# Two of the first loads issued by ScalarE, and one warm-up matmul fewer

## The chip, the cores and the metric

The kernel runs on one core of a Trainium2 chip. The metric is the device time of one execution in microseconds (us), smaller is better. A difference is told in per cent of the time before.

## What is computed

`x` is 2048 x 512. The output mixes two branches of `x`, row by row, with a gate. All of it is float32.

```
g = sigmoid((x * gate_w).sum(-1))
# branch A: real part of a DFT along the hidden and the sequence dimension
a = x @ dft_hid_re.T;  b = x @ dft_hid_im.T
A = dft_seq_re @ a - dft_seq_im @ b
# branch B: a gated MLP with ReLU, 512 -> 1792 -> 512
B = (relu(x @ W_gate) * (x @ W_up)) @ W_down
out = g * A + (1 - g) * B
```

## The kernel before

Every float32 operand is split in a high and a low part, and a product is made of three matmuls (high by low, low by high, high by high), each 128 x 128 by 128 x 512. Most products go through a scheme of seven half-size products per 2 x 2 block product. Only the first block of the MLP is multiplied directly (class `Direct`), so that its matmuls need little preparation. In the trace these matmuls write `c` from `xb11h`, `xb11l`, `xb21h` and so on (parts of `x`) and from `wf0h`, `wf0l`, `wf1h`, `wf1l` (parts of the first weight tile; 0 and 1 are the two values of `d`).

The program is recorded first. Each step gets a key, which is its due place in the row of matmuls. A planner then decides in which order each engine runs its steps, and which of 51 SBUF units each buffer gets. TensorE (PE) runs its matmuls in the order written. VectorE (DVE) and ScalarE (ACT) may take steps out of turn by due time, and so may the queue of SyncE (SP), which issues the loads. The planner reckons with a queue for each engine that issues DMAs.

The head of the program is what the change touches. PE runs `WARM` matmuls on a memset tile (`warm`, which has no other use) while the first data are loaded. SP issues `x` "11" (two pieces, `k` 0 and 1, 256 KB each) and the first weight tile `wf` with `d` 0 (two pairs of 128 KB for each `k`), in the order x, wf, wf, x, wf, wf, and then the pieces for `d` 1. VectorE casts each piece of x "11" to `xb11h` and subtracts to get `xb11l`. ScalarE casts each pair of `wf` to `wf0h`, and VectorE subtracts to get `wf0l`. The first real matmul needs `xb11h` and the first pair of `wf0h`, both for `k` 0. The third and fourth need the second pair, and the next four need `xb11l`.

Of the kernel before, what the change touches and what calls it, by code (L numbers as in the profile page):

```python
# [344 lines left out]
def kernel(ctx: ExitStack, tc, xP, xG, wf, wgu, wd, cr, ci, wri, gw, out):  # L345
# [27 lines left out]
    plan = Plan()  # L373
# [20 lines left out]
    def buf(name, shape=(2, N), dtype=F32):  # L394
        return Buf(plan, name, list(shape), dtype)
# [22 lines left out]
    def mm(ps, w, x, start=False, stop=False):  # L418
        plan.tensor.matmul(ps, w, x, start=start, stop=stop, skip_group_check=True)
# [7 lines left out]
    def load(o, i):  # L427
        plan.sync.dma_start(o, i)
# [187 lines left out]
    class Direct:  # L616
# [32 lines left out]
                   start=first, stop=d == k == 1 and n == 2)  # L649

        def w_load(self, d, k, s=slice(0, 4)):
            load(self.raw[d][:, k, s], wf[d, :, k, s])

        def w_hi(self, d, k, s=slice(0, 4)):
            E().scalar.copy(self.w[d][0][:, k, s], self.raw[d][:, k, s])
# [624 lines left out]

    WARM = 8
    warm, wp = buf("warm", [P], F32R), Pair("warm")

    def warm_up():
        E().vector.memset(f32(warm.all), 1.0)
        wp.new()
        for n in range(WARM):
            mm(wp[0], warm.all, warm.all.unsqueeze(1).to_broadcast([P, N // P, P]), start=n == 0, stop=n == WARM - 1)  # L1290

# [180 lines left out]
```

## Time and profile before

| | |
|---|---|
| time, median of 3 runs | 783.7 us (783.29 to 783.92) |
| time of the profiled execution | 783.86 us |
| its span (first to last instruction) | 782.1 us |
| PE busy | 777.5 us, 99% of the span |
| VectorE, ScalarE, GpSimd busy | 89%, 52%, 15% |

The time is 1.76 us more than the span in the profiled execution. The matmul engine is busy for all but 4.6 us of the span: about 1 us ahead of the first matmul, and about 3.5 us behind the last one, in which the last results are copied and stored.

### The profile page before, as it was taken

The numbers are of one execution on the slowest core, as the hardware profiler recorded it, in microseconds if no ns is written. First come the engines' busy times: TensorE is split into PE (matmuls) and PEld (weight loads), VectorE is DVE, ScalarE is ACT, GpSimd is POOL, SyncE is SP. The second block draws the span as 40 slices with busy tenths as digits, with TensorE's granted clock in tenths as the row PEclk, the third lists the DMA queues.
The fourth block names the chain that finished last, engine by engine and source line by source line (L and its number), as shares of the span: only waits on it lengthen the run. The fifth ranks groups of instructions, "written<-read, shape, count | busy, mean of one in ns | idle before, by whom it ended". The sixth has DMA issues, their size and how long they took to land.

```text
span 782.1 us, 9936 instructions
## 1 busy us (share of the span) xinstructions
PE 777.5 (99%) x3428; PEld 644.0 (82%) x3428; DVE 698.4 (89%) x795; ACT 406.2 (52%) x537; POOL 115.2 (15%) x181
## 2 busy tenths in 40 slices
PE   9999999999999999999999999999999999999998
PEld 7888888888888888888888888888888888888886
DVE  6999999999999654899997799987999999989896
ACT  5643322222234112464656576576679857645762
POOL 0101322232222112011110000100100002012010
PEclk9999999999999999999999999999999999999999
DMA  8623999999996699589999999989999998997954
GB/s 318 259 95 121 324 404 414 418 325 419 419 396 199 230 338 419 219 302 382 415 417 408 380 313 359 310 281 343 331 390 412 410 358 206 325 238 217 327 156 108
DMA packets 71891, 248.41 MB, mean 318 GB/s; under 512 B 8224, under 2 KB 8992, under 8 KB 71840
## 3 DMA queue, kind: packets, MB, share of 16 engines
q1 hardware_dynamic: 47360, 159.02, 54.1%
q0 software_dynamic: 24336, 88.62, 33.6%
q8 instruction: 27, 0.44, 0.2%
q14 instruction: 24, 0.20, 0.1%
q10 hardware_dynamic: 144, 0.13, 0.1%
HBM read 165.94 MB, written 81.80 MB: 317 GB/s over the span
## 4 chain that ended last, share of the span: by engine, by line
PE 99%; ACT 0%; issue 0%; DVE 0%; ACTq 0%
PE z L127 45%; PE c L127 35%; PE a L127 10%; PE jB L127 3%; PE jA L127 3%; PE jX L127 1%; PE jD L127 1%; PE jG L127 1%; PE warm L127 0%; PE jH L127 0%; ACT jo L127 0%; DVE warm L127 0%; ACTq L127 0%
## 5 line engine op out<-in xcount | busy, mean ns | idle before, releaser
L127 PE MATMUL z<-ch,ll 128*128 128x512 f32 x516 | 200.7, 389 | 0.0
L127 PE MATMUL z<-cl,lh 128*128 128x512 f32 x516 | 200.7, 389 | 0.0
L127 PE MATMUL z<-ch,lh 128*128 128x512 f32 x516 | 200.7, 389 | 0.0
L127 PEld LDWEIGHTS z<-ch,lh 128*128 128x128 f32 x516 | 96.9, 188 | 20.2
L127 PEld LDWEIGHTS z<-ch,ll 128*128 128x128 f32 x516 | 96.9, 188 | 20.0
L127 PEld LDWEIGHTS z<-cl,lh 128*128 128x128 f32 x516 | 96.9, 188 | 20.0
L127 ACT CAST ch<-r 128x1024 fp32r<-128x1024 f32 x80 | 82.5, 1053 | 57.3 <-DVE r L127 43.1
L127 DVE TENSOR_TENSOR cl<-r,ch 128x1024 fp32r<-128x1024 f32 x80 | 96.3, 1220 | 8.2 <-ACT ch L127 6.4
L127 DVE TENSOR_TENSOR cl<-hr,ch 128x1024 fp32r<-128x1024 f32 (+1 forms) x56 | 60.1, 1087 | 11.8 <-ACT ch L127 7.5
L127 DVE TENSOR_TENSOR jcl<-jr,jch 128x1024 fp32r<-128x1024 f32 x56 | 67.2, 1221 | 3.4 <-PE z L127 1.5
L127 ACT CAST ch<-hr 128x1024 fp32r<-128x1024 f32 (+1 forms) x56 | 52.0, 945 | 31.6 <-DMA hr<-hd 11.1
L127 ACT CAST jch<-jr 128x1024 fp32r<-128x1024 f32 x56 | 57.7, 1054 | 5.3 <-DVE jcl L127 2.5
L127 DVE TENSOR_TENSOR p<-p,p 128x1024 f32<-128x1024 f32 x44 | 53.4, 1220 | 0.3
L127 DVE TENSOR_TENSOR r<-r,r 128x1024 f32<-128x1024 f32 x39 | 47.0, 1219 | 3.5 <-DMA r<-cr 3.5
L127 ACT ACTIVATE c<-c 128x512 f32<-128x512 f32 x26 | 15.1, 582 | 66.8 <-PE c L127 66.8
L127 ACT COPY z<-z 128x512 f32<-128x512 f32 x56 | 31.6, 586 | 21.2 <-PE z L127 18.7
L127 PE MATMUL c<-xh,wb0l 128*128 128x512 f32 x104 | 40.5, 389 | 0.0
L127 PE MATMUL c<-xl,wb0h 128*128 128x512 f32 x104 | 40.5, 389 | 0.0
L127 PE MATMUL c<-xh,wb0h 128*128 128x512 f32 x104 | 40.5, 389 | 0.0
L127 PE MATMUL c<-xh,wb1l 128*128 128x512 f32 x104 | 40.5, 389 | 0.0
L127 PE MATMUL c<-xl,wb1h 128*128 128x512 f32 x104 | 40.5, 389 | 0.0
L127 PE MATMUL c<-xh,wb1h 128*128 128x512 f32 x104 | 40.5, 389 | 0.0
(237 smaller groups left out, 1541.1 us busy)
## 6 DMA issues: line engine op xcount, KB each, us to landing
tb<-p POOLq DMA_DIRECT2D x44, 512.0 KB, 10.1
hr<-hd SPq DMA_DIRECT2D x42, 512.0 KB, 9.2
p<-cr SPq DMA_DIRECT2D x36, 512.0 KB, 7.7
jr<-tb SPq DMA_DIRECT2D x32, 512.0 KB, 9.1
hd<-hs POOLq DMA_DIRECT2D x28, 512.0 KB, 8.1
r<-ci SPq DMA_DIRECT2D x24, 512.0 KB, 8.7
l<-ad SPq DMA_DIRECT2D x20, 512.0 KB, 8.7
jr<-cr SPq DMA_DIRECT2D x18, 512.0 KB, 8.8
```

The source lines that it names most:

```text
L127: getattr(getattr(nc, self.engine), self.name)(*map(ap, self.a), **{k: ap(x) for k, x in self.k.items()})
```

## The change

The loads of the first weight tile with `d` and `k` 0 (two DMAs of 128 KB) are issued by ScalarE. The other loads stay with SyncE. `WARM` is 7 in place of 8.

```diff
         def w_load(self, d, k, s=slice(0, 4)):
-            load(self.raw[d][:, k, s], wf[d, :, k, s])
+
+            (plan.scalar if d == k == 0 else plan.sync).dma_start(self.raw[d][:, k, s], wf[d, :, k, s])
...
-    WARM = 8
+    WARM = 7
```

The order of the rows below is that of the built program, engine by engine. On SyncE at the start of the program (`x_80` is x "11", `wf_84` the weight tile for `d` 0, `x_97` x "21", `wf_101` the weight tile for `d` 1) before:

```order
L127 DMA x_80<-xP 128x512
L127 DMA wf_84<-wf 128x256 x2
L127 DMA x_80<-xP 128x512
L127 DMA wf_84<-wf 128x256 x2
L127 DMA x_97<-xP 128x512
L127 DMA wf_101<-wf 128x512
```

and now, where the same tiles are `x_80`, `wf_82`, `x_96` and `wf_98`:

```order
L127 DMA x_80<-xP 128x512 x2
L127 DMA wf_82<-wf 128x256 x2
L127 DMA x_96<-xP 128x512
L127 DMA wf_98<-wf 128x512
L127 DMA x_96<-xP 128x512
L127 DMA wf_98<-wf 128x512
```

The first two loads of the weight tile have left the row, so every load behind the first moved up by two places.

On ScalarE at the start of the program, now:

```order
L127 DMA wf_82<-wf 128x256 x2
L127 ACT_TABLE_LOAD
L127 CAST wf0h<-wf_82 128x256 x4
L127 CAST xb21h<-x_96 128x512
L127 CAST wf1h<-wf_98 128x512
```

Before, the row began with the table load. The two issues now stand ahead of it and of all casts.

The planner, which sees other times at the head, also moves some steps near the block that uses the second half of `x` for the first time. On VectorE, in the program's third and fourth block (`xs` are sums of pieces of `x`, `xl` low parts, `c` PSUM banks, `h`, `u`, `g` parts of the MLP's hidden layer), before:

```order
L127 TENSOR_TENSOR xs_510<-x_198,x_190 128x1024
L127 TENSOR_TENSOR xs_520<-x_204,x_194 128x1024
L127 TENSOR_TENSOR xl_529<-xs_503,xh_516 128x1024
L127 TENSOR_TENSOR t<-c,t 128x512 x2
L127 TENSOR_TENSOR xl_548<-xs_510,xh_524 128x1024
L127 TENSOR_TENSOR h_555<-g,c 128x512
```

and now:

```order
L127 TENSOR_TENSOR xs_508<-x_199,x_189 128x1024
L127 TENSOR_TENSOR xl_518<-xs_499,xh_511 128x1024
L127 TENSOR_TENSOR t<-c,t 128x512 x2
L127 TENSOR_TENSOR xl_535<-xs_508,xh_522 128x1024
L127 TENSOR_TENSOR xs_544<-x_203,x_193 128x1024
L127 TENSOR_TENSOR h_551<-g,c 128x512
```

One sum of `x` moved behind two low parts and a pair of evacuations. Five steps of VectorE and five of ScalarE change their places in this way, all of them in these blocks. Behind them the rows of all engines are the same as before, up to buffer numbers, and so is the tail.

## Rows read from the trace of the kernel before

**Rows 1.** The chain that ended last, in order of time (start us, us, what).

```profile
0.84 0.18 DVE warm L127
1.02 0.04 issue
1.06 3.78 PE warm L127 x8
4.85 232.28 PE c L127 x1020
...
775.69 2.88 PE jH L127 x24
...
778.65 0.37 ACT jo L127
```

**Rows 2.** All waits of PE and of its weight load (total, times, longest, us).

```profile
PE warm L127 <- DVE warm L127: 1.1, 1, 1.1
...
PEld c L127 <- ACT wf0h L127: 0.3, 1, 0.3
```

**Rows 3.** Timeline of PE in narrow windows: start us, us, instruction; ends overlap.

```profile
1.06 3.78 PE L127 MATMUL warm<-warm 128*128 128x512 f32 x8 [1.06 <-DVE warm L127]
...
4.22 0.63 PE L127 MATMUL warm<-warm 128*128 128x512 f32 x1
...
4.64 1.91 PE L127 MATMUL c<-xb11h,wf0h 128*128 128x512 f32 x4
6.35 1.39 PE L127 MATMUL c<-xb11l,wf0h 128*128 128x512 f32 x4
...
6.78 0.73 PE L127 MATMUL c<-xb11l,wf0h 128*128 128x512 f32 x2
...
7.11 0.62 PE L127 MATMUL c<-xb11l,wf0h 128*128 128x512 f32 x2
...
7.57 1.07 PE L127 MATMUL c<-xb11h,wf0l 128*128 128x512 f32 x4
8.48 1.07 PE L127 MATMUL c<-xb11h,wf0h 128*128 128x512 f32 x4
```

**Rows 4.** Timeline of the head on SP's queue, VectorE and ScalarE.

```profile
0.75 0.38 SPq L127 DMA_DIRECT2D x<-xP  x1
1.19 0.89 SPq L127 DMA_DIRECT2D wf<-wf  x2
2.12 0.43 SPq L127 DMA_DIRECT2D x<-xP  x1
...
0.74 1.28 ACT L127 ACT_TABLE_LOAD   x1 [0.74 <-PEq L1465]
...
3.39 0.43 DVE L127 CAST xb11h<-x 128x512 fp32r<-128x512 f32 x1 [2.38 <-DMA x<-xP]
...
3.98 0.88 ACT L127 CAST wf0h<-wf 128x256 fp32r<-128x256 f32 x2 [1.95 <-DMA wf<-wf]
```

**Rows 5.** Timeline of the weight load: the first real one, and the first of `wf1h`.

```profile
4.43 1.40 PEld L127 LDWEIGHTS c<-xb11h,wf0h 128*128 128x128 f32 x4 [0.31 <-ACT wf0h L127]
...
10.98 0.64 PEld L127 LDWEIGHTS c<-xb21h,wf1h 128*128 128x128 f32 x3
```

**Rows 6.** Half microseconds of the head: busy time by engine, PEclk, DMA share, GB/s.

```profile
1.50:2.00 0.50, 0.50 (x2) 0.40 (x2) 0.00 (x0) 0.50 (x1) 0.00 (x0) 1.00 0.35 41
2.00:2.50 0.50, 0.50 (x2) 0.33 (x1) 0.00 (x0) 0.02 (x1) 0.00 (x0) 1.00 0.86 315
2.50:3.00 0.50, 0.50 (x3) 0.40 (x2) 0.00 (x0) 0.00 (x0) 0.00 (x0) 1.00 0.90 324
3.00:3.50 0.50, 0.50 (x3) 0.41 (x2) 0.11 (x1) 0.00 (x0) 0.00 (x0) 1.00 0.62 172
```

**Rows 7.** ScalarE, timeline: the cast of `wf1h` in the head.

```profile
9.60 0.62 ACT L127 CAST wf1h<-wf 128x512 fp32r<-128x512 f32 x1
```

**Rows 8.** Timeline where the planner moved steps: ScalarE, PE and VectorE.

```profile
67.16 0.58 ACT L127 ACTIVATE c<-c 128x512 f32<-128x512 f32 x1 [5.41 <-PE c L127]
67.66 1.05 ACT L127 CAST xh<-x 128x1024 fp32r<-128x1024 f32 x1
...
71.05 0.39 PE L127 MATMUL c<-xh,wa0l 128*128 128x512 f32 x1
...
65.61 0.39 PE L127 MATMUL c<-xh,wa0l 128*128 128x512 f32 x1
...
58.32 1.22 DVE L127 TENSOR_TENSOR xl<-xs,xh 128x1024 fp32r<-128x1024 f32 x1
```

**Rows 9.** The only load or store that ScalarE issues: its time, size and landing.

```profile
779.05 0.37 ACTq L127 DMA_DIRECT2D out<-jo  x1
...
out<-jo ACTq DMA_DIRECT2D x1, 128.0 KB, 2.0
```

## The prediction

> **What bounds the kernel now.** I read the chain of waits first, from its end back to its start. It is one engine: a memset on VectorE, eight warm-up matmuls, then matmuls without a break up to 778.57 us, and a copy and a store behind them [rows 1]. The list of waits says the same from the other side: in the whole span PE waited once, for the memset, and its weight load once more, 0.31 us for `wf0h`, which the last warm-up matmul covered [rows 2, 5]. So the time is the start of the first real matmul, plus the number of matmuls by their spacing, plus a tail of 3.5 us. Only what moves the first of these, the speed at which the head runs, or what opens a gap later can move the time.
>
> The narrow timeline of PE then gives two spacings. From the warm-ups up to the matmul at 6.78 us they start 0.427 us apart (4.22 to 4.64, and 4.64 to 6.35 in four steps); 512 columns in 0.427 us is the 1.2 GHz level. From 7.57 to 8.48 four starts are 0.227 us apart, close to the 2.4 GHz level. The step from 6.78 to 7.11, 0.33 us, is half of each, so the rise lies near 7.0 us [rows 3]. The granted-clock column stands at 1.00 through the head [rows 6] and does not show this; the spacing does. PE had been fed without a break from 1.06 us until then.
>
> **The change, part by part.** *One warm-up less.* It frees one slot of 0.427 us: the seventh is issued at 3.79 us, and the first real matmul could start at 4.22 in place of 4.64 [rows 3]. It is real work only if its operands are there.
>
> *The two issues on ScalarE.* SP needs 0.38 us for the issue of x and 0.89 us for the two of `wf` [rows 4]; the one issue that ScalarE makes in the trace took 0.37 us [rows 9]. ScalarE was free at 0.74 us, when its table load began. Now it issues two loads until about 1.5 us, and the table load of 1.28 us ends near 2.8. It was waiting for `wf` until 3.98 anyway, so I cost the move of the table load at nothing. That cover is gone only if `wf` lands before 2.8 us, when nothing is late. On SP all later loads go out about 0.9 us earlier (2.12 becomes 1.19 for the second piece of x).
>
> *When can the first matmul start?* x was issued at 0.75 and its cast began at 3.39, 2.64 us later; `wf` was issued at 1.19 and its cast began at 3.98, 2.79 us later [rows 4]. If both keep these, x is cast at 3.39 + 0.43 = 3.82, and `wf`, issued at 0.74, is cast at 3.53 and ready at 3.53 + 0.44 = 3.97. The weight load could go at 3.98 and the matmul 0.21 us behind it, as before (4.43 to 4.64), so at 4.19. It would then wait for the seventh warm-up and start at 4.22. That is the early bound.
>
> The late bounds take the transfers as competing. While x moves, the DMA engines are busy 86 to 90% at 315 to 324 GB/s; only then, from 3.0 to 3.5, is there slack (62%, 172 GB/s) [rows 6]. At 320 GB/s the first pair of 131 thousand bytes takes 0.41 us. If it goes wholly ahead of part of x, x is ready at 4.23 and the first matmul starts at 4.45. If both pairs push in, it is 4.64 us and the start 4.86. Since x has twice the bytes and the queues should share, I take a start near 4.35, between the early bound and one pair of delay.
>
> The Trainium skill weighs against the early bound: "DMA: Bandwidth & Descriptors", section "Issuing engines are not separate DMA queues", says that loads issued by several engines run on the same 16 DMA engines and interleave, and that only the sequencer's time to issue is saved. The half microseconds agree in part: busy at 86 to 90% first, then a gap. By the rule alone, without that gap, the loads for `k` 0 would be complete no earlier than before, and the sum would be nothing.
>
> *What an earlier start is worth.* Not its full length. If the clock rises at the same 7.0 us, the matmuls ahead of the rise still go at 0.427 us, and what is gained is matmuls that need not be run behind it, at 0.227 us each. A start earlier by s gives s / 0.427 x 0.227 = 0.53 s: for 4.22 it is 0.22 us, for 4.35 it is 0.15, for 4.45 it is 0.10, and for 4.86 a loss of 0.12. If the rise came forward with the start, all of 0.42 us would be gained; no row speaks for that.
>
> *Nothing else late in the head?* PE then wants each later tile 0.2 us earlier. The closest is `wf1h`: its cast ends at 9.60 + 0.62 = 10.22 and its weight load starts at 10.98, 0.76 us later [rows 5, 7]. Its loads also go out earlier. I cost this at nothing; without that slack it would cost at most the same 0.2 us.
>
> *The planner's moves.* Five steps each of VectorE and ScalarE swap places near 50 to 80 us. On ScalarE a cast of 1.05 us now stands ahead of the copy `c<-c` at 67.16, which had waited 5.41 us for PE. It ends at 67.74 and the matmul that needs that bank starts at 71.05, so there are 3.3 us for one cast. The third of VectorE's low parts ends at 59.54, and the first matmul with any of the second half of `x` starts at 65.61, 6.1 us later [rows 8]. A swapped sum of 1.22 us fits in. I cost this at nothing, and if the slack were not there a swap would cost at most that 1.22 us, once.
>
> **The sum.** In the profiled execution PE's stream ends 0.15 us earlier: span 782.1 to 781.95, time 783.86 to 783.7. That execution is 0.16 us above the median of the runs, so by the median it is 783.7 - 0.15 = 783.55; I say 783.5. That is 0.02%, far inside the 0.2% (1.57 us) that a measurement of this kernel can tell from no change.
>
> **The rivals.**
> *Nothing moves.* The loads share the DMA engines, x lands as much later as `wf` lands earlier, and PE stands idle where the eighth warm-up was. For it: the 86 to 90% while x moves. Against it: the slack at 3.0 to 3.5. A start anywhere from 4.6 to 4.9 gives 783.7 to 783.8. The page above is the rule behind this rival. 20%.
>
> *The full slot.* The clock rises as much earlier as the work starts: 783.3. Nothing speaks for it but that the trace shows only one rise. 8%.
>
> *Slower: the gap delays the clock.* Before, PE had been fed from 1.06 us until the rise near 7.0, 5.9 us. With seven warm-ups there may be a hole between 4.2 us and the first real matmul, and after it the low level might last longer. Each microsecond of later rise costs 1 - 0.227 / 0.427 = 0.47 us. As a place to price it I take the first weight load of `wf1h` at 10.98 us [rows 5], where the second half of the direct products begins: a rise there, 4.0 us late, costs 1.9 us, less the 0.1 gained: 785.5. It would be slower by over 0.2% from a rise 3.6 us late on, at about 10.6 us. Against it: by the early bound there is no hole, and by the next 0.2 us. 5%, of which I put three beyond the bound.
>
> *Slower: a gap in the stream* in the head or at the planner's swaps, 1.22 us or more, 784.8 to 786. Against it: the slacks of 3.3 and 6.1 us. 4%, three of them beyond the bound.
>
> **How the numbers follow.** The forecast (start at 4.22 to 4.45) has 61%, nothing moved 20, the full slot 8, a later clock 5, a gap 4, and 2% for a faster head by over 0.2%: the whole low-level stretch from 1.06 to 7.0 costs 0.47 x 5.9 = 2.8 us, so an earlier rise could give as much. The runs of before alone spread over 0.63 us. The range of 782.8 to 784.5 holds the first three cases with that spread on both sides, and leaves out the rest. Faster by over 0.2%: 2%; within it: 92%; slower: 6%.
>
> **What would show it.** The changed kernel's PE timeline should have seven warm-ups 0.427 us apart, the first `c` at 4.2 to 4.5 us, spacing 0.427 up to about 7.0 us, and a last matmul some 0.1 to 0.2 us earlier. ScalarE's queue should show two issues from 0.74 us, and the casts of `xb11h` and `wf0h` should begin at 3.4 to 3.8 us. The list of waits should hold no wait of PE but the memset and at most one of 0.2 us for `xb11h` or `wf0h`. A first `c` behind 4.6 us means that the loads compete; 0.427 us spacing far behind 7 us means the clock; any wait of PE at 50 to 80 us means the planner.

## The result and the profile after

The change made the kernel slower: 785.93 us (median of 10 runs, 784.22 to 788.08) against 783.73 (10 runs, 782.90 to 784.60). The ratio is 1.0028, with a 95% interval from 1.0017 to 1.0039. The runs also scatter more: over 3.9 us, where those of before scatter over 1.7. The profiled execution of the changed kernel took 784.22 us and was the fastest of the ten, so it shows only part of the loss. The rest has to be found by experiment.

The chain that ended last (start us, us, what) now begins with the moved loads, where it began with the memset and the warm-ups [rows 1]:

```profile
0.74 0.41 ACTq L127
1.16 0.03 issue
1.19 4.78 DMA wf<-wf
5.96 0.02 issue
5.98 0.41 ACT wf0h L127
6.40 0.04 issue
6.44 231.06 PE c L127 x1018
...
779.02 0.37 ACT jo L127
```

The second pair of the weight tile is issued at 1.19 us and its cast starts at 5.98. From 6.44 on PE runs as before, and no wait at the planner's swapped steps appears. The last copy starts at 779.02 us against 778.65 [rows 1]; these 0.37 us are the whole loss of this execution (784.22 against 783.86 us). All waits of PE in the whole span (total, times, longest):

```profile
PE c L127 <- ACT wf0h L127: 1.3, 2, 1.0
PE warm L127 <- DVE warm L127: 1.1, 1, 1.1
```

The head in the timeline of the changed kernel, first the loads and casts, then PE:

```profile
0.74 0.89 ACTq L127 DMA_DIRECT2D wf<-wf  x2
0.74 0.86 SPq L127 DMA_DIRECT2D x<-xP  x2
...
1.67 1.28 ACT L127 ACT_TABLE_LOAD   x1 [1.67 <-PEq L1466]
...
4.80 0.43 DVE L127 CAST xb11h<-x 128x512 fp32r<-128x512 f32 x1 [3.80 <-DMA x<-xP]
...
4.97 0.40 ACT L127 CAST wf0h<-wf 128x256 fp32r<-128x256 f32 x1 [2.03 <-DMA wf<-wf]
...
1.06 3.36 PE L127 MATMUL warm<-warm 128*128 128x512 f32 x7 [1.06 <-DVE warm L127]
...
5.43 0.74 PE L127 MATMUL c<-xb11h,wf0h 128*128 128x512 f32 x2 [1.02 <-ACT wf0h L127]
...
6.44 0.73 PE L127 MATMUL c<-xb11h,wf0h 128*128 128x512 f32 x2 [0.27 <-ACT wf0h L127]
...
7.01 1.09 PE L127 MATMUL c<-xb11l,wf0h 128*128 128x512 f32 x4
```

The reader is to see three things against [rows 3, 4]. The cast of x starts at 4.80 us in place of 3.39, though x is issued when it was. The cast of the first pair starts at 4.97 in place of 3.98, though it is issued 0.45 us earlier. And PE has two holes, of 1.02 and 0.27 us, where before the warm-ups ran into the first real matmul. The first pair of real matmuls takes 0.74 us, ends included, against 1.06 for a pair at 0.427 us spacing: in this execution the clock had risen by 5.43 us, so the holes cost little here.

The half microseconds of the same stretch as [rows 6] (last two columns: DMA share, GB/s):

```profile
2.00:2.50 0.50, 0.50 (x2) 0.33 (x1) 0.00 (x0) 0.50 (x1) 0.00 (x0) 1.00 0.81 211
2.50:3.00 0.50, 0.50 (x3) 0.40 (x2) 0.00 (x0) 0.45 (x1) 0.00 (x0) 1.00 0.65 180
3.00:3.50 0.50, 0.50 (x3) 0.41 (x2) 0.00 (x0) 0.00 (x0) 0.00 (x0) 1.00 0.76 215
```

and the two queues apart from 2.5 to 3.0 us (packets, MB, share of 16 engines; q1 is SyncE's, q10 ScalarE's):

```profile
q10 hardware_dynamic: 32, 0.03, 35.0%
q1 hardware_dynamic: 28, 0.06, 30.3%
```

In 1.5 us some 0.30 MB are moved, against 0.41 before; and SyncE's queue, with x in front, gets only a part of them.

### The profile page after: what moved, and what is told of

Its sections match the earlier page's. It is cut to its first block, busy times and chain, and to the rows that moved or that the text cites. A ratio compares the mean times of both kernels' runs of the same rounds, so it can differ in the third digit from the quotient of the medians.

```text
span 782.5 us, 9934 instructions
## 1 busy us (share of the span) xinstructions
PE 776.6 (99%) x3427; PEld 642.6 (82%) x3427; DVE 698.1 (89%) x795; ACT 407.1 (52%) x537; POOL 115.4 (15%) x181
## 4 chain that ended last, share of the span: by engine, by line
PE 99%; DMA 1%; ACT 0%; ACTq 0%; issue 0%
PE z L127 45%; PE c L127 34%; PE a L127 10%; PE jB L127 3%; PE jA L127 3%; PE jX L127 1%; PE jD L127 1%; PE jG L127 1%; DMA wf<-wf 1%; PE jH L127 0%; ACTq L127 0%; ACT wf0h L127 0%; ACT jo L127 0%
```

## Theories and experiments

Clock theory: two loads side by side land late, PE has holes behind the warm-ups, and in most executions the holes put off the rise of the clock. Landing theory: the late first matmul is the whole loss. Planner theory: the ten swapped steps cost it. Beside the first four kernels, before took 783.89 us (33 runs, 782.74 to 785.12).

**The two parts alone, and the holes filled.** Three kernels differ from the changed one or from before in the number of warm-ups alone, one is the other part of the change alone. The order of all other steps is that of the kernel named.

```diff
 changed kernel:  WARM = 7 -> 8     (loads on ScalarE, eight warm-ups)
 before:          WARM = 8 -> 7     (loads on SyncE, seven)
 changed kernel:  WARM = 7 -> 10    (loads on ScalarE, ten)
 before:          WARM = 8 -> 5     (loads on SyncE, five)
```

> The two loads on ScalarE as in the changed kernel, eight warm-ups as before. Theories. Clock theory: the loads land late, PE has holes of 0.8 and 0.3 us behind the warm-ups, and in most executions the holes put off the rise of the clock, 0.47 us for each microsecond. Landing theory: the late first matmul alone is the loss, and the clock rises near 7 us all the same. Planner theory: the steps that changed places cost it. By clock theory the eighth warm-up takes 0.43 us of the first hole of 0.8: between 784.2 and 786, nearer to 785, still with a wide spread. By landing theory nothing changes against seven warm-ups in the profiled execution, 784.2, and the median stays where the changed kernel's is, 785.9. By planner theory 785.9, since the order of the steps is that of the changed kernel.

Measured: 784.75 us (784.04 to 786.57), ratio 1.0015 (1.0006 to 1.0024). One warm-up more takes 1.2 us off the median of the changed kernel. The median hides two groups: five of the eleven runs lie at 784.04 to 784.21, five at 785.79 to 786.57, and one at 784.75. Of the changed kernel's ten runs two lie at 784.22 and 784.31, and the rest at 785.35 to 788.08.

> All loads on SyncE as before, seven warm-ups. The loads land as before, the first matmul starts near 4.64 us, and a hole of 0.43 us stands where the eighth warm-up was; the order of all other steps is that of before. Clock theory: the hole puts off the rise in some executions, so 783.7 to 785.0 with a wider spread than before. Landing theory and planner theory: 783.7, as before.

Measured: 783.71 us (783.18 to 786.40), ratio 1.0002 (0.9993 to 1.0011). The median does not move, but three of eleven runs lie at 785.05 to 786.40. All three theories allow this median. In the profile the first real matmul starts at 4.51 us and PE's list shows no wait ahead of it.

> The two loads on ScalarE, ten warm-ups, which last until 5.9 us and cover the first hole and most of the second. The loads land as late as in the changed kernel. Clock theory: the rise comes near 7 us in every execution, so 784.2 to 784.6, with a spread below 1.5 us. Landing theory: PE's real work starts at 5.9, not earlier than with seven, so no gain: 785.9 in the median. Planner theory: 785.9.

Measured: 784.12 us (784.00 to 784.45), ratio 1.0003 (0.9994 to 1.0012). This decides. The loads land as late as in the changed kernel (its casts start at 4.81 and 5.00 us), the steps stand in the changed kernel's order, and three matmuls on a tile that nobody reads make it 1.8 us faster and shrink the scatter from 3.9 to 0.45 us. Its PE timeline:

```profile
1.05 4.25 PE L127 MATMUL warm<-warm 128*128 128x512 f32 x10 [1.05 <-DVE warm L127]
...
4.91 0.40 PE L127 MATMUL warm<-warm 128*128 128x512 f32 x1
...
5.45 0.73 PE L127 MATMUL c<-xb11h,wf0h 128*128 128x512 f32 x2
...
6.44 0.73 PE L127 MATMUL c<-xb11h,wf0h 128*128 128x512 f32 x2 [0.26 <-ACT wf0h L127]
```

Ten warm-ups take 4.25 us, only 0.47 more than eight did [rows 1], since the clock rose during them. Of the first hole 0.15 us are left (5.30 to 5.45), and the second of 0.26 us stays. Landing and planner theory both wanted 785.9. It also speaks against loads that land later still in the longer executions of the changed kernel: ten warm-ups end at 5.30 us, so that such loads would show here as well, and all eleven runs lie within 0.45 us.

> All loads on SyncE as before, five warm-ups, which end near 3.4 us; a hole of 1.2 us up to the first real matmul at 4.64. The loads land as before and the order of the steps is that of before. Clock theory: the rise is late by some microseconds in most executions: 784.8 to 786.5. Landing theory and planner theory: 783.7 to 783.8, since the first real matmul starts when it did.

Measured: 785.70 us (784.64 to 786.33), ratio 1.0020 (1.0011 to 1.0029). This is the counterpart: no load and no other step is moved, only a hole is made, and the loss is nearly that of the change. The profiled execution (786.33 us) shows it:

```profile
1.06 2.50 PE L127 MATMUL warm<-warm 128*128 128x512 f32 x5 [1.06 <-DVE warm L127]
5.23 2.07 PE L127 MATMUL c<-xb11h,wf0h 128*128 128x512 f32 x4 [1.67 <-ACT wf0h L127]
7.11 1.91 PE L127 MATMUL c<-xb11l,wf0h 128*128 128x512 f32 x4
...
8.81 1.71 PE L127 MATMUL c<-xb11h,wf0l 128*128 128x512 f32 x4
10.36 1.08 PE L127 MATMUL c<-xb11h,wf0h 128*128 128x512 f32 x4
11.28 1.07 PE L127 MATMUL c<-xb11l,wf0h 128*128 128x512 f32 x4
```

The groups of four start 1.70 us apart from 7.11 to 8.81, four times 0.427, and 0.92 us apart from 10.36 on. The 1.2 GHz level lasts to about 10 us, where before it ended near 7 [rows 3]. One thing is not as meant: in this execution the first pair of `wf` landed 0.8 us later than before, so the hole was 1.67 us and not 1.2.

Not all that this execution loses is lost in the head. Two pieces of the chain that ended last, the starts of two later stretches of matmuls (on `a` and `z`), first before, then with five warm-ups, then in the run below that holds back SyncE's later loads:

```profile
237.13 76.16 PE a L127 x336
...
351.37 176.80 PE z L127 x780
```

```profile
239.01 76.16 PE a L127 x336
...
353.75 176.80 PE z L127 x780
```

```profile
238.90 76.16 PE a L127 x336
...
353.14 176.80 PE z L127 x780
```

With five warm-ups PE is 1.88 us late behind the head and 2.38 us late at 353.75. The 0.50 us between are a wait of PE at 330 us for `h`, a part of the hidden layer, which VectorE computes late. In the same chain, and in the list of PE's waits:

```profile
329.66 0.61 DVE h L127
330.27 0.04 issue
330.31 23.44 PE c L127 x102
```

```profile
PE c L127 <- DVE h L127: 0.2, 1, 0.2
```

VectorE is late because some 10 us earlier it waited 3.2 us for a load (`wd`), where before it waited 1.5. PE's list has the wait for `h` in two more of the fourteen profiled executions, that of seven warm-ups on SyncE's loads (0.5 us) and that of the crossed run below (0.4 us). It is a second source of scatter; why that load is late there was not tested. In the run that holds SyncE's later loads back, all of the 1.77 us are lost in the head.

**The changed kernel again.** Two more profiles of it, with nothing changed.

> The changed kernel once more, for a second profile. The first profiled execution was the fastest of ten (784.22 against a median of 785.93). Clock theory: an execution near the median shows the same holes behind the seven warm-ups and a spacing of 0.427 us that lasts some 3 us beyond 7 us. Landing theory: it shows the 0.227 us spacing from 7 us on, and loads that land up to 2 us later still.

> The changed kernel a third time, for the profile of an execution near the median of 785.9, since the first two profiled ones took 784.22 and 784.14. Clock theory: near the median, a spacing of 0.427 us that lasts to about 10 us; an execution at 784.2 shows the rise during or right behind the warm-ups.

Measured: 784.14 and 784.24 us. Both profiled executions lie at the low end again, with holes of 0.94 and 0.25, and of 1.02 and 0.22 us, and with 0.23 us from matmul to matmul right behind. So no profile of the changed kernel near its median was had.

**Why do the loads land late?** Two theories: two queues at once are slow, or a load issued by ScalarE is slow by itself. The first kernel holds back all of SyncE's loads behind the first piece of x, by writes of VectorE on their buffers. The second leaves one pair on SyncE.

```diff
+    def hold():
+        v, z = plan.vector, piece[0, "11"]
+        v.tensor_copy(z[:, 1, 0:1], f32(warm[:, 0:1]))
+        for _ in range(3):
+            v.memset(z[:, 1], 0.0)
...
+        for t in later:
+            v.tensor_copy(t, z[:, 1, 0:1])
...
-            (plan.scalar if d == k == 0 else plan.sync)
+            (plan.scalar if d == k == s.start == 0 else plan.sync)
```

> The changed kernel, with three memsets and some small copies on VectorE, idle there, that keep SyncE from issuing any load behind the first piece of x until about 2.5 us. For a while only the first piece of x and the two pairs on ScalarE are in flight. If sharing the DMA engines with SyncE's later loads made the first operands late, x lands near 3.5 to 3.8 us and the pairs by 4.4, the first matmul starts at 4.2 to 4.6, and the time is 783.5 to 784.3. If a load issued by ScalarE is slow by itself, the pairs land at 4.9 and 5.9 as in the changed kernel and the time stays near 785.9.

Measured: 784.55 us (783.53 to 785.74), ratio 1.0005 (0.9997 to 1.0014), where before took 783.99 (29 runs) beside it. SyncE's next load goes out at 3.38 us, later than meant. x lands at about 4.4 us (3.7 from issue) and the pairs at about 4.6 and 4.8 (3.9 and 3.6): earlier than in the changed kernel, and between the two theories' numbers. So SyncE's later loads are a part of the delay, about 0.35 us for x; x and the two pairs, on two queues, are late by themselves. Before, these three loads landed one after another, at about 3.4, 4.0 and 4.4 us; side by side none of them lands before the last one did then. The profiled execution (785.68 us) had a hole of 0.67 us and the low level again to about 10 us:

```profile
5.08 2.08 PE L127 MATMUL c<-xb11h,wf0h 128*128 128x512 f32 x4 [0.67 <-ACT wf0h L127]
6.95 1.91 PE L127 MATMUL c<-xb11l,wf0h 128*128 128x512 f32 x4
...
8.66 1.72 PE L127 MATMUL c<-xb11h,wf0l 128*128 128x512 f32 x4
10.22 1.09 PE L127 MATMUL c<-xb11h,wf0h 128*128 128x512 f32 x4
```

> Only the first pair of the weight tile on ScalarE, the second back on SyncE behind the first piece of x; seven warm-ups. If sharing makes the landings late, half the sharing gives half the delay: x near 4.0 us, the first matmul at 4.6 to 5.1, the time 784 to 785. If ScalarE's loads are slow by themselves, the first pair lands at 4.9 us as in the changed kernel, and the time is 785 to 786.

Measured: 785.53 us (783.15 to 786.24), ratio 1.0013 (1.0003 to 1.0024). The cast of x starts at 4.21 us and the first real matmul at 4.85, as the sharing theory had it. The time lies above its range and inside that of the other theory, 785 to 786, but the cast of the first pair starts at 4.39 us, not at 4.9. The profiled execution was the fastest of twelve: a hole of 0.42 us, and the clock up all the same. A hole makes a late rise likely, not certain.

The next two carry the first piece of x over: in one ScalarE issues x and both pairs, with SyncE held back as above; in the other ScalarE issues x alone and SyncE all else.

```diff
-        load(piece[q, b][:, ks], xP[2 * q + j, k, :, ks])
+        (plan.scalar if (q, b, ks.start) == (0, "11", 0) and ks.stop == 1 else plan.sync).dma_start(
+            piece[q, b][:, ks], xP[2 * q + j, k, :, ks])
```

> As the run that held SyncE's later loads back, and the first piece of x is issued by ScalarE too, ahead of the two pairs: for a while one queue alone moves the same three loads that SyncE moved before the change. That run gave x at 4.43 us and the first pair by 4.59. If two queues at once are what is slow, these land here as before the change: x near 3.4 to 3.5 us, the pairs near 4.0 and 4.4. If ScalarE's queue is slow by itself, x lands near 4.4 us or later.

> Crossed over: ScalarE issues the first piece of x, SyncE the weight tile and all else; seven warm-ups. If two queues at once delay both, x lands between 4.2 and 4.9 us and the first pair between 4 and 4.9. If ScalarE's queue is slow by itself, x lands at 4.8 us or later and the first pair, first on SyncE now, at 3.4 to 3.6.

Measured, one run each: 784.06 and 786.13 us. With ScalarE's queue alone, x landed 2.6 us after its issue and the first pair 2.9, as on SyncE's queue before (2.6 and 2.8 [rows 4]). Half microseconds of that run:

```profile
2.00:2.50 0.50, 0.50 (x2) 0.33 (x1) 0.48 (x1) 0.39 (x1) 0.00 (x0) 1.00 0.93 344
2.50:3.00 0.50, 0.50 (x3) 0.40 (x2) 0.33 (x2) 0.50 (x1) 0.00 (x0) 1.00 0.89 295
3.00:3.50 0.50, 0.50 (x3) 0.40 (x2) 0.47 (x6) 0.40 (x1) 0.00 (x0) 1.00 0.67 207
```

That is the pattern of before [rows 6], with the other queue. Crossed over, x on ScalarE took 3.6 us and the pairs on SyncE 3.4 to 3.5: both late, whichever queue has which. So two queues at once are what makes x late, and ScalarE's queue by itself is not slow. Whether the second queue does it, or only that x no longer goes ahead of the pairs, these two profiles do not tell apart. That the table load lies beside the transfers makes no difference either: it ran from 2.11 to 3.39 us beside those 2.6 to 2.9 us loads. The crossed run's profile has a hole of 0.53 us and the low level to about 9.4 us; of the 2.2 us that it is longer than before, 1.43 are lost in the head and the rest at 330 us.

**A better version.** The same result suggests that before itself has executions with a late rise; none was caught in a profile. More warm-ups on the kernel before, `WARM = 10` and `WARM = 9`:

> All loads on SyncE as before, ten warm-ups. The operands are there at 4.43 us and wait for the tenth warm-up, 0.85 us behind the eighth. Clock theory: no hole in any execution, two matmuls more at 0.227 us each where the clock rises at the same time: 784.0 to 784.4, with a spread below 1 us against 2.4 of before. Without it, 0.85 us of later start: 784.7, with the spread of before.

> All loads on SyncE, nine warm-ups: between before (eight) and the run with ten, which took 783.61 against 783.99. Clock theory: the first real matmul at about 5.1 us, no hole if the first pair is cast by then, 783.5 to 783.9 with a spread below that of before. A difference from before that can be told is not expected.

Measured: ten, 783.61 us (783.14 to 784.40) against 783.99 (782.69 to 785.70), ratio 0.9994 (0.9986 to 1.0003); nine, 783.39 us (782.82 to 784.00) against 783.65 (782.73 to 786.67), ratio 0.9993 (0.9985 to 1.0002). Both beat the changed kernel. Against before neither difference can be told, though the scatter is smaller in both (1.26 and 1.18 us in 11 and 12 runs, against 3.0 and 3.9 in 29 and 17).

## Why the prediction was wrong

The direction, the range and the mechanism of the forecast were all wrong; of its rivals, the one at 5% came out.

**When the first matmul can start** is the first step that failed. I took 4.35 us, between 4.22 and 4.86; it was 5.43, and 6.44 for the third matmul. My bounds delayed x alone and left the first pair's cast at 3.53 us; it began at 4.97, and it was for this pair that PE waited, while the second pair, which I gave no term, made the hole at 6.44. My latest bound let both pairs of `wf` go ahead of x at 320 GB/s. But that rate belonged to one queue at work: in the changed kernel 180 to 215 GB/s were moved from 2.0 to 3.5 us. I also left out that SyncE's second piece of x, which goes out 0.93 us earlier, joins in; the run that held it back puts that at some 0.35 us. The page of the Trainium skill that I set against the early bound ("DMA: Bandwidth & Descriptors", section "Issuing engines are not separate DMA queues") had the sense of it, that the loads interleave and that ScalarE's gain nothing but issue time. The runs agree and go further than it says: x landed 3.4 to 4.0 us after issue with two queues, and 2.6 to 2.7 with one.

**The clock that rises at 7.0 us** is the second. I read that from one execution and held it fixed. The profiles show it near 4.7 us in the run with ten warm-ups on late loads, by 5.43 in the changed kernel, near 7.0 before, and about 10 in two runs with a hole. With that, my rule that a start earlier by s gives 0.53 s had no firm ground, and the rival that I gave 5%, *slower: the gap delays the clock*, became the likeliest case. Its price was well sized: 0.47 us for each microsecond of later rise, 785.5 for 4.0 us. I argued against it from my own landing times (no hole, or one of 0.2 us), which were wrong.

The loss can be split, as an estimate. The three profiled executions of the changed kernel, with an early rise, took 784.1 to 784.2 us, 0.4 to 0.5 more than the median of before: that is the late start, less what a rise earlier than the 7.0 us of before's profile gave back. (The fastest execution with one pair on ScalarE, which started at 4.85 us with the clock up, took 783.15.) From there to the median of 785.9 it is 1.7 us, which at 0.47 is a rise some 3.6 us later. The slowest run, 788.08, would ask for some 8 us, which no profile shows. That the holes are the cause of these 1.7 is shown by filling them (784.12, on the same late loads) and by making one without touching any load (785.70). That it is the clock is seen in three runs with holes, most plainly where all 1.77 us are lost in the head, but not in the changed kernel itself, whose executions near the median were not caught in a profile. Why two queues moved fewer bytes in the changed kernel (0.30 MB from 2.0 to 3.5 us, but 0.39 with one pair on ScalarE) also stays open.

**What held.** The table load behind the issues cost nothing: it ended at 2.95 us, 2.0 us before the cast. The swapped steps of the planner cost nothing that can be seen: no wait of PE at 50 to 80 us, and ten warm-ups with those same swaps take 784.12 us. No other tile of the head made PE wait.

## What to carry to other kernels

A matmul on a dummy tile looks like waste in a timeline, but the stretch from the first matmul to the rise of the clock is worth keeping full: cover the latest time at which the first operands can land, not the one seen in one profile, because a warm-up too many cost nothing measurable here (nine, ten) and a hole cost 1.8 us in the median (five). Where the first work waited for a few small loads, one queue in the order of need had the first of them there 0.7 us or more earlier than two queues at once. And where runs scatter more after a change, ask which kind of execution the profile shows before taking any event's time from it.

## What was not expected of the hardware

In the profiles with the first loads on one queue, x (256 KB) landed 2.6 to 2.7 us after issue, and 3.4 to 4.0 us when both queues were at work. The first 128 KB pair took 2.8 to 2.9 us on one queue in four profiles, but 3.3 and 3.6 us in two others (nine and five warm-ups), so its lateness alone does not tell the two cases apart; with both queues it took 3.4 to 4.2 us, and the second pair up to 4.8. In the changed kernel 0.30 MB were moved in 1.5 us in place of 0.41. The rise to the 2.4 GHz level came anywhere from 4.7 to 7.0 us in executions in which PE was fed without a break from 1.06 us. With holes it came near 10 us in some, and in others as early as without: by 5 us behind a hole of 0.42 us, and by 5.43 behind one of 1.02 us.
